# A fused attention and two-layer kernel: fixed places for all SBUF tiles, and tiles of their own for one batch's remaining keys and values

## The chip, the cores and the metric

The kernel runs on one core of one Trainium2 chip. The metric is device time in microseconds (us) for one execution. The core's engines are TensorE (PE, with its weight loads shown apart as PEld), VectorE (DVE), ScalarE (ACT), GpSimd (POOL) and SyncE (SP). Here SP issues all transfers between HBM and SBUF.

## The reference

The reference is linear attention with a norm, followed by two two-layer blocks, all in float32. The shapes are 8 batches, 8 heads, 576 positions and head size 64, and then 4608 tokens, model width 512 and hidden width 2048.

```python
kv = np.einsum('bhsd,bhse->bhde', k, v)
out = np.einsum('bhsd,bhde->bhse', q, kv)
rms = np.sqrt(np.mean(out * out, axis=-1, keepdims=True) + 1e-06)
x = (out / rms * g_norm)            # then to (4608, 512)
h = x @ w_in1;  g = h * (1.0 / (1.0 + np.exp(-1.702 * h)));  y = g @ w_out1
h = y @ w_in2;  r = np.maximum(h, 0.0);  out = (s * (r * r) + b) @ w_out2
```

## The kernel before, in words

Every float32 operand of the large products is split into a high and a low part (`xh`, `xl`; `wih`, `wil`; `gh`, `gl`; the two halves of `wo`), and three matmuls (high by high, low by high, high by low) stand for one product. The three have lines of their own: L424 to L426 in the first layer's first product (`mm1`), L453 to L455 in its second (`mm2`), L520 to L522 and L616 to L618 in the second layer. In each of these matmuls the first-named SBUF operand in the code is the stationary one (loaded as weights, 128 columns) and the second the moving one (512 columns).

**First layer.** The 4608 tokens are nine blocks of 512. A step of the main loop (`for n in range(2, ...)`, L931) takes one of 16 slices of the hidden width for one block: 12 matmuls of `mm1` on the block's transposed input, then 12 matmuls of `mm2` of the step two before. Blocks 0 and 1 alternate in parts at the beginning, while their weights come in; the others take 16 steps each. A block's input lies in `xh0` and `xl0` if its number is even and in `xh1` and `xl1` if it is odd (`x_tiles`, L337). Beside these steps the attention of the next block runs: `kv_pair` (keys by values, L222), `att_u` (queries, L297), the norm and the transposition of four tiles of 128 tokens; `tile_at` (L662) says in which step each part of a tile stands.

**Second layer.** The second layer's first product is done by a scheme with seven block products in place of eight (`product`, L507). It works on 4 couples of blocks and one single block, each in 8 pairs of hidden slices. Its weights are the stationary operand. They are loaded in halves that go round `xh1`, `xl1`, `xl0` (`load_half`, L489), and the moving operand is in the tiles that held `wih` and `wil`, or in `xh0`. Between the products stand the second product's matmuls (`units`, L594): stationary is the activation, which lies in places listed in `G_PLACE` (for pairs of even number `wraw`, `kt`, `vt`; for pairs of odd number `q`, `xn0` and `xn1`, `wf0` and `wf1`, `gh`), moving is `wo`. A pair has 42 matmuls of the first kind and 48 of the second.

**The beginning, written out by hand (L764 to L921).** For each batch the first 512 positions of keys and values come as four pairs of tiles (`load_kv`, L211), the other 64 as one pair of tiles `krem`, `vrem` (`load_rem`, L205), of which there is one pair for all batches. All transfers go through SP in the order in which they are written. `kv_pair` multiplies a pair's four chunks and then the remaining rows. Batch 0's four pairs (`kv_first`) end with the remaining rows, so `load_rem(1)` stands behind the last of them, at L808, after the loads of batch 1's four pairs. `kv_pair(1, 0)` stands at L832, and behind it on PE the transposition of the third tile (`att_turn(2)`), on ACT `x_first(2)`, on DVE `xl_first(2)`. From L763 on `keep_warm` puts matmuls of no use into gaps.

**Where the tiles lie.** Tiles of the pool `sb` lie one behind the other in each partition, in the order in which their names are first taken in the program. A tile of 512 numbers has 2048 bytes per partition, the larger ones 4096 or 8192; `ms0` to `ms3` and `r0` to `r3` have 8 numbers, 32 bytes. The names are first taken in this order: `kt0 vt0 q0 kt1 vt1 q1 wraw0 yf0 yf1 yf4 yf2 yf3 yf5 wraw1 xn0 | ms0 r0 | wf0 xn1 | ms1 r1 | xh0 xl0 xo0 xo1 wst wc yf6 wf1 | ms2 r2 ms3 r3 | wih0 wil0 wf2 wih1 wil1 g0 wo0 gh0 xh1 xl1 g1 gl0 ...` and then all others. So, counted in bytes beyond a multiple of 256 from the first tile, `kt0` to `xn0` start at 0, `wf0` and `xn1` at 64, `xh0` to `wf1` at 128, and all from `wih0` on, `xh1` and `xl1` among them, at 0 again. The slices that the large matmuls read are multiples of 256 bytes into their tiles.

Of the kernel before, what the change touches and what calls it, by code (L numbers as in the profile page):

```python
# [16 lines left out]
P = 128  # L17
B, H, S, D = 8, 8, 576, 64
# [4 lines left out]
BT = 512  # L23
NB = NT // BT
TT = BT // P
# [2 lines left out]
CUTS = (0, 2, 6, 11, KF)  # L28
HEAD = [(j, lo, hi) for lo, hi in zip(CUTS, CUTS[1:]) for j in range(2)]
PARTS = HEAD + [(j, 0, KF) for j in range(2, NB)]  # L30
WARM = 8
SM = 512
NC = SM // P
# [9 lines left out]
def tile_attn_moe_moe2(  # L43
# [18 lines left out]
    nc = tc.nc  # L62
# [7 lines left out]
    def new(tag, shape=(P, BT), dtype=F32, name=None):  # L70

        return sb.tile(list(shape), dtype, tag=tag, name=name or tag)

    def rot(tag, n, shape=(P, BT), dtype=F32, name=None):

        turns[tag] = turns.get(tag, -1) + 1
        return new(f"{tag}{turns[tag] % n}", shape, dtype, name or tag)

    def move(dst, src):

        raw = [x.bitcast(F32) if x.dtype == F32R else x for x in (dst, src)]
        nc.sync.dma_start(out=raw[0], in_=raw[1])
# [14 lines left out]
    rem_t = {nm: const.tile([P, H * D], F32, name=f"{nm}rem") for nm in "kv"}  # L97
# [7 lines left out]
    def load_w(which, ph, f):  # L105
        raw = rot("wraw", 2, (P, DM, 2), U32)
        nc.sync.dma_start(out=raw.rearrange("p a b -> p (a b)"), in_=w_arg[ph][which][f].bitcast(U32))
        w_raw[which, ph, f] = raw

    def to_f32(which, ph, f):  # L110

        raw = w_raw.pop((which, ph, f))
        lo, hi = raw[:, :, 0], raw[:, :, 1]
        w = rot("wf", 3, (P, DM), U32)
        nc.scalar.activation(out=w.bitcast(F32), in_=hi.bitcast(F32), func=ACTF.Abs)
        nc.scalar.activation(out=lo, in_=lo, func=ACTF.Copy, scale=2.0 ** -29)
        yield

        nc.vector.tensor_scalar(
            out=w.bitcast(F32), in0=w.bitcast(F32), scalar1=W_LEAST, scalar2=W_MOST, op0=ALU.max, op1=ALU.min
        )
        yield
        nc.vector.tensor_scalar(
            out=w, in0=w, scalar1=3, scalar2=0x3FFFFFF8, op0=ALU.logical_shift_left, op1=ALU.bitwise_and
        )
        yield
        nc.vector.scalar_tensor_tensor(
            out=w, in0=hi, scalar=0xC0000000, in1=w, op0=ALU.bitwise_and, op1=ALU.bitwise_or  # L130
        )
        yield
        nc.vector.tensor_tensor(out=w, in0=w, in1=lo, op=ALU.add)
        w_raw[which, ph, f] = w.bitcast(F32)
        yield
# [66 lines left out]

    kt, vt, rem = {}, {}, {}

    def load_rem(bb):  # L205
        for nm, src in (("k", k_rest), ("v", v_rest)):

            nc.sync.dma_start(out=rem_t[nm][0:S - SM], in_=src[bb])
            rem[nm, bb] = rem_t[nm]

    def load_kv(bb, p, place=None):  # L211
        for nm, src, dst, hl in (("kt", k, kt, 0), ("vt", v, vt, 1)):
            if place is None:
                t = rot(nm, 2, (P, NC, P))
            else:
                t = new(place[hl], (P, NC, P))
            nc.sync.dma_start(out=t, in_=src[bb, p].rearrange("p (c e) -> p c e", e=P))
            dst[bb, p] = t
# [66 lines left out]
    def load_q(i, place=None):  # L285
        if place is None:
            q_t[i] = rot("q", 2, (P, NP, P))
        else:
            q_t[i] = new(place, (P, NP, P))
        nc.sync.dma_start(out=q_t[i], in_=q[i].rearrange("p (a t) -> p a t", t=P))  # L290
# [20 lines left out]
    def att_sq(i, place=None):  # L311
        if place is None:
            xn_t[i] = rot("xn", 2, (P, H, D))
        else:
            xn_t[i] = new(place, (P, H, D))
        nc.scalar.activation(out=xn_t[i], in_=u_t[i], func=ACTF.Square, scale=D ** -0.5)
# [43 lines left out]
    y_dram = {}  # L360
    for j, lo, _ in PARTS:
        y_dram.setdefault(j, {})[lo] = dp.tile([KD, P, BT], F32, name=f"y{j}_{lo}")
# [44 lines left out]

    steps = [(j, f, lo, hi) for j, lo, hi in PARTS for f in range(lo, hi)]
    begin = {}
# [245 lines left out]
    def at(n, slot, fn, *args):  # L655
        beside.setdefault((n, slot), []).append((fn, args))
# [5 lines left out]
    def tile_at(i, n, n_norm, n_turn, slot="turn"):  # L662

        at(n, "pe", att_u, i)
        at(n, "act", att_sq, i)
        at(n, "r", att_r, i)
        at(n_norm, "norm", att_norm, i)
        at(n_turn, slot, att_turn, i)
        early = "0" if slot == "pe" else ""
        at(n_turn, "xh" + early, att_xh, i)  # L670
        at(n_turn, "xl" + early, att_xl, i)
# [10 lines left out]
    def next_kv(bb, n):  # L682
        at(n, "load", load_rem, bb)
        for p in range(2):
            at(n, "load", load_kv, bb, p)

    at(5, "load", load_rem, 2)
    for p in range(2):
        at(7 + 2 * p, "load", load_kv, 2, p)

    n0 = begin[1, CUTS[-2]]
# [4 lines left out]
    tile_at(2 * TT, n0 - 2, n0 - 1, n0, "pe")  # L696
    tile_at(2 * TT + 1, n0 - 1, n0, n0)
    tile_at(2 * TT + 2, n0 + 1, n0 + 2, n0 + 2)
    tile_at(2 * TT + 3, n0 + 1, n0 + 2, n0 + 2)

    for v_ in range(3, NB):
        n0 = begin[v_ - 1, 0]
# [37 lines left out]
    for n in range(2 * KF, NB * KF):  # L740
        j, f = divmod(n, KF)
# [5 lines left out]
            at(n - RING + 2, "load", load_wo, 0, f)  # L747

    with tc.manual_schedule():
        make_identity(nc, ident)  # L750
        for t in rem_t.values():
            nc.gpsimd.memset(t[S - SM:P], 0.0)
        for t in kvbd:
            nc.gpsimd.memset(t, 0.0)
# [5 lines left out]
        def keep_warm(n):  # L760
            for _ in range(n):
                nc.tensor.matmul(o[:, 0:P], ident, ident, start=True, stop=True)

        keep_warm(WARM)  # L764
        load_kv(0, 0)
        load_rem(0)
        load_q_pair(0, "q0")
        load_kv(0, 1)
# [21 lines left out]
        keep_warm(5)  # L790
        next(ci0)
        att_sq(1, xn_place[1])
        load_kv(1, 0)
        load_kv(1, 1)
        kv_first(2)
# [9 lines left out]
        u_first(2)  # L805
        load_kv(1, 2, ("xo0", "xo1"))
        load_kv(1, 3, ("wst", "wc"))
        load_rem(1)  # L808
        load_q(4)
        load_q(5)  # L810
        kv_first_out(3)
# [253 lines left out]
```

## Time and profile before

| what | value |
|---|---|
| three runs | 1650.14 us median (1649.44 to 1652.71) |
| the profiled execution | 1650.09 us |
| its span, first to last instruction | 1648.3 us |
| PE busy | 1631.0 us (99%), 8008 matmuls |
| DVE, ACT, POOL busy | 912.1 us (55%), 665.3 us (40%), 68.7 us (4%) |
| the chain that ended last, by engine | PE 95%, DMA 2%, DVE 1%, ACT 1% |
| granted TensorE clock, mean | 0.996 |
| transfers | 375.75 MB, mean 228 GB/s |

The profile has one line for each group of instructions; in `out<-in` the buffers' numbers are left out, so `xl` is `xl0` or `xl1`. PE busy counts a matmul from its start to its modelled end; these overlap, so the pace of the engine is read from the starts. The granted clock is 1.00 at 2.4 GHz and 0.50 at 1.2 GHz.

### The profile page before, as it was taken

The numbers are of one execution on the slowest core, as the hardware profiler recorded it, in microseconds if no ns is written. First come the engines' busy times: TensorE is split into PE (matmuls) and PEld (weight loads), VectorE is DVE, ScalarE is ACT, GpSimd is POOL, SyncE is SP. The second block draws the span as 40 slices with busy tenths as digits, with TensorE's granted clock in tenths as the row PEclk, the third lists the DMA queues.
The fourth block names the chain that finished last, engine by engine and source line by source line (L and its number), as shares of the span: only waits on it lengthen the run. The fifth ranks groups of instructions, "written<-read, shape, count | busy, mean of one in ns | idle before, by whom it ended". The sixth has DMA issues, their size and how long they took to land.

```text
span 1648.3 us, 21336 instructions
## 1 busy us (share of the span) xinstructions
PE 1631.0 (99%) x8008; PEld 1343.7 (82%) x8008; DVE 912.1 (55%) x1520; ACT 665.3 (40%) x1164; POOL 68.7 (4%) x47
## 2 busy tenths in 40 slices
PE   8999999999999999999999999999999999999999
PEld 6788788888888888888888888888888888888888
DVE  5876636656666545665534655555455455445443
ACT  4665533443444433443323433333333333333343
POOL 3000100001000000100000000000000000000000
PEclk9999999999999999999999999999999999999999
DMA  6566757687787766776588844974486448544773
GB/s 230 188 227 199 243 178 248 238 298 267 270 300 294 275 211 222 251 269 210 190 316 281 312 155 167 317 243 153 142 288 222 140 142 292 191 140 142 251 278 140
DMA packets 126775, 375.75 MB, mean 228 GB/s; under 512 B 14417, under 2 KB 20049, under 8 KB 121169
## 3 DMA queue, kind: packets, MB, share of 16 engines
q1 hardware_dynamic: 126672, 374.40, 65.2%
q8 instruction: 63, 1.03, 0.3%
q14 instruction: 40, 0.32, 0.1%
HBM read 284.69 MB, written 89.65 MB: 227 GB/s over the span
## 4 chain that ended last, share of the span: by engine, by line
PE 95%; DMA 2%; DVE 1%; ACT 1%; issue 0%; SPq 0%; ACTq 0%; DVEq 0%
PE acc L453 8%; PE h L424 8%; PE h L426 8%; PE acc L455 8%; PE h L425 8%; PE acc L454 8%; PE sum L616 4%; PE sum L617 4%; PE sum L618 4%; PE A L520 4%; PE A L521 4%; PE A L522 4%; PE z L618 4%; PE z L616 4%; PE z L617 4%; PE D L522 2%
## 5 line engine op out<-in xcount | busy, mean ns | idle before, releaser
L453 PE MATMUL acc<-gh,wo 128*128 128x512 f32 x576 | 230.0, 399 | 1.0 <-ACT ev L463 1.0
L424 PE MATMUL h<-xh,wih 128*128 128x512 f32 x576 | 229.1, 398 | 0.0
L426 PE MATMUL h<-xl,wih 128*128 128x512 f32 x576 | 226.5, 393 | 0.0
L425 PE MATMUL h<-xh,wil 128*128 128x512 f32 x576 | 226.1, 393 | 0.0
L455 PE MATMUL acc<-gl,wo 128*128 128x512 f32 x576 | 225.5, 391 | 0.0
L454 PE MATMUL acc<-gh,wo 128*128 128x512 f32 x576 | 225.4, 391 | 0.0
L431 ACT ACTIVATE g<-h 128x512 f32<-128x512 f32 x144 | 86.0, 597 | 274.2 <-PE h L426 273.9
L432 DVE TENSOR_TENSOR g<-g,h 128x512 f32<-128x512 f32 x144 | 98.8, 686 | 162.5 <-ACT g L431 162.2
L436 ACT CAST gh<-g 128x512 fp32r<-128x512 f32 x144 | 89.5, 622 | 138.1 <-DVE g L432 138.1
L453 PEld LDWEIGHTS acc<-gh,wo 128*128 128x128 f32 x576 | 108.8, 189 | 25.0 <-ACT ev L463 1.4
L426 PEld LDWEIGHTS h<-xl,wih 128*128 128x128 f32 x576 | 108.4, 188 | 24.7
L425 PEld LDWEIGHTS h<-xh,wil 128*128 128x128 f32 x576 | 108.6, 188 | 23.3
L455 PEld LDWEIGHTS acc<-gl,wo 128*128 128x128 f32 x576 | 108.6, 188 | 23.2
L424 PEld LDWEIGHTS h<-xh,wih 128*128 128x128 f32 x576 | 108.4, 188 | 22.7
L454 PEld LDWEIGHTS acc<-gh,wo 128*128 128x128 f32 x576 | 108.7, 189 | 21.5
L440 DVE TENSOR_TENSOR gl<-g,gh 128x512 fp32r<-128x512 f32 x144 | 98.9, 687 | 27.3 <-PE acc L455 26.2
L323 POOL TENSOR_TENSOR r<-ms,mhalf 128x8 f32<-128x8 f32 x36 | 66.0, 1838 | 721.6 <-DVE ms L322 721.6
L565 DVE TENSOR_TENSOR wst<-B,wst 128x512 f32<-128x512 f32 (+1 forms) x40 | 25.5, 639 | 108.2 <-PE B L522 108.1
L520 PE MATMUL A<-wih,xl 128*128 128x512 f32 (+1 forms) x212 | 78.7, 371 | 0.2 <-ACT wst L562 0.2
L522 PE MATMUL A<-wil,xl 128*128 128x512 f32 (+1 forms) x212 | 78.5, 370 | 0.0
L521 PE MATMUL A<-wih,xl 128*128 128x512 f32 (+1 forms) x212 | 78.4, 370 | 0.0
L626 DVE TENSOR_TENSOR g<-z,g 128x512 f32<-128x512 f32 x56 | 38.7, 692 | 56.4 <-PE z L618 55.8
(241 smaller groups left out, 3144.6 us busy)
## 6 DMA issues: line engine op xcount, KB each, us to landing
wo<-wo SPq DMA_DIRECT2D x208, 512.0 KB, 4.9
x<-xo SPq DMA_DIRECT2D x56, 512.0 KB, 4.0
xl<-wi SPq DMA_DIRECT2D x26, 1024.0 KB, 5.3
xl<-wi SPq DMA_DIRECT2D x27, 768.0 KB, 4.7
wraw<-in_w_in SPq DMA_DIRECT2D x32, 512.0 KB, 4.5
wraw<-in_w_out SPq DMA_DIRECT2D x32, 512.0 KB, 4.2
y<-ev SPq DMA_DIRECT2D x60, 256.0 KB, 2.7
yf<-y SPq DMA_DIRECT2D x60, 256.0 KB, 5.1
```

Of the source, the lines that this page charges most:

```text
L424: nc.tensor.matmul(o, wh[:, cs], xh[:, c, :], start=(c == 0), stop=False)
L425: nc.tensor.matmul(o, wl[:, cs], xh[:, c, :], start=False, stop=False)
L426: nc.tensor.matmul(o, wh[:, cs], xl[:, c, :], start=False, stop=(c == KD - 1))
L453: nc.tensor.matmul(o, wh[:, ds_], gh, start=(f == lo), stop=False)
L454: nc.tensor.matmul(o, wl[:, ds_], gh, start=False, stop=False)
L455: nc.tensor.matmul(o, wh[:, ds_], gl, start=False, stop=(f == hi - 1))
L520: nc.tensor.matmul(o, wh, xh, start=(c == 0 and not more), stop=False, skip_group_check=more)
L521: nc.tensor.matmul(o, wl, xh, start=False, stop=False, skip_group_check=more)
L522: nc.tensor.matmul(o, wh, xl, start=False, stop=(c == 1), skip_group_check=more)
L616: nc.tensor.matmul(o, gh[:, cs], wh, start=begins, stop=False)
L617: nc.tensor.matmul(o, gh[:, cs], wl, start=False, stop=False)
L618: nc.tensor.matmul(o, gl[:, cs], wh, start=False, stop=ends)
```

## The change

A list `PLACES` names all tiles of the pool, and a new function takes each of them once, at the beginning and in this order. The eight small tiles stand together in it, behind `wf0` and ahead of `xh0`. Batch 1's remaining rows go to two new tiles in the places of `ev0` and `ev1` (free until the first partial result is written), are cleared beside the old pair on POOL, and are loaded ahead of batch 1's first pair rather than behind its last. The fourth tile of block 2 (`2 * TT + 3`) has its `att_u`, norm and transposition one step later each.

```diff
+PLACES = (
+    "kt0 vt0 kt1 vt1 yf0 yf1 yf2 yf3 q0 q1 wraw0 yf4 yf5 wraw1 xo0 xo1 wst wc xn0 xn1 yf6 wf0 "
+    "ms0 r0 ms1 r1 ms2 r2 ms3 r3 xh0 xl0 wih0 wil0 wf1 wih1 wil1 wf2 g0 gh0 wih2 wil2 g1 gh1 "
+    "wo0 gl0 xh1 xl1 wih3 wil3 gl1 gh2 wo1 wo2 wo3 ev0 ev1 ev2 ev3 wih4 wil4 wih5 wil5 wih6 wil6 "
...
+    def lay_out():
+        sizes = {"wraw": 1024, "xo": 1024, "wst": 1024, "wc": 1024, "wo": 1024, "xh": 2048, "xl": 2048, "ms": H, "r": H}
+        for tag in PLACES.split():
+            new(tag, (P, sizes.get(tag.rstrip("0123456789"), BT)))
...
-    def load_rem(bb):
+    def load_rem(bb, place=rem_t):
         for nm, src in (("k", k_rest), ("v", v_rest)):
-            nc.sync.dma_start(out=rem_t[nm][0:S - SM], in_=src[bb])
-            rem[nm, bb] = rem_t[nm]
+            nc.sync.dma_start(out=place[nm][0:S - SM], in_=src[bb])
+            rem[nm, bb] = place[nm]
...
-    tile_at(2 * TT + 3, n0 + 1, n0 + 2, n0 + 2)
+    tile_at(2 * TT + 3, n0 + 2, n0 + 3, n0 + 3)
...
     with tc.manual_schedule():
+        lay_out()
         make_identity(nc, ident)
-        for t in rem_t.values():
+        rem_t1 = {nm: new(f"ev{i}", (P, H * D), name=f"{nm}rem1") for i, nm in enumerate("kv")}
+        for t in (*rem_t.values(), *rem_t1.values()):
             nc.gpsimd.memset(t[S - SM:P], 0.0)
...
         att_sq(1, xn_place[1])
+        load_rem(1, rem_t1)
         load_kv(1, 0)
...
         load_kv(1, 3, ("wst", "wc"))
-        load_rem(1)
         load_q(4)
```

## Rows read from the trace of the kernel before

**Rows 1.** Windows: us, busy of PE, PEld, DVE, ACT, POOL, clock, DMA share, GB/s.
```profile
24.50:31.30 6.80, 5.09 (x34) 4.07 (x35) 2.77 (x5) 1.91 (x3) 0.00 (x0) 0.50 0.41 140
```

**Rows 2.** Timeline of PE: start, us, instruction, count, idle before and its releaser.
```profile
21.39 0.69 PE L236 MATMUL kvps<-vt,kt 128*64 128x64 f32 x16
26.21 0.48 PE L236 MATMUL kvps<-vrem,krem 128*64 128x64 f32 x4 [4.14 <-DMA vrem<-in_v_rest]
...
64.64 0.50 PE L453 MATMUL acc<-gh,wo 128*128 128x512 f32 x1 [0.98 <-ACT ev L463]
```

**Rows 3.** Timeline of SP's queue: batch 1's first keys, the remaining values, first output weights.
```profile
12.94 0.33 SPq L217 DMA_DIRECT2D kt<-in_k  x1
...
20.23 0.48 SPq L208 DMA_DIRECT2D vrem<-in_v_rest  x1
...
22.55 0.33 SPq L107 DMA_DIRECT2D wraw<-in_w_out  x1
```

**Rows 4.** DMA view, transfers issued at 13.69 and 22.55: KB, us to landing.
```profile
vt<-in_v SPq DMA_DIRECT2D x1, 256.0 KB, 6.5
...
wraw<-in_w_out SPq DMA_DIRECT2D x1, 512.0 KB, 5.9
```

**Rows 5.** Timelines of DVE and of ACT behind the late rows.
```profile
28.50 0.75 DVE L281 SCALAR_TENSOR_TENSOR xl<-xtp,g,xh 128x512 fp32r<-128x512 f32 x1 [3.61 <-ACT xh L276]
...
32.87 0.75 DVE L281 SCALAR_TENSOR_TENSOR xl<-xtp,g,xh 128x512 fp32r<-128x512 f32 x1 [1.96 <-ACT xh L276]
...
28.45 0.68 ACT L117 ACTIVATE wf<-wraw 128x512 f32<-128x512 f32 x1
```

**Rows 6.** Timeline of POOL: a clear of 64 rows, and the four norms of block 1.
```profile
1.83 0.52 POOL L752 MEMSET vrem<- 64x512 f32 x1
...
38.46 6.64 POOL L323 TENSOR_TENSOR r<-ms,mhalf 128x8 f32<-128x8 f32 x4 [14.41 <-DVE ms L322]
```

**Rows 7.** Timeline of PE: `mm1`'s first matmul and `mm2`'s, blocks 4 and 5.
```profile
471.04 0.40 PE L424 MATMUL h<-xh,wih 128*128 128x512 f32 x1
...
473.83 0.39 PE L453 MATMUL acc<-gh,wo 128*128 128x512 f32 x1
...
568.35 0.39 PE L424 MATMUL h<-xh,wih 128*128 128x512 f32 x1
...
571.07 0.39 PE L453 MATMUL acc<-gh,wo 128*128 128x512 f32 x1
```

**Rows 8.** Timeline of PE: six matmuls with weights in `xl1`, six in `xl0`.
```profile
1082.55 0.39 PE L520 MATMUL A<-wih,xl 128*128 128x512 f32 x1
...
1083.91 0.39 PE L616 MATMUL sum<-wo,wraw 128*128 128x512 f32 x1
...
1092.08 0.40 PE L520 MATMUL A<-wih,xl 128*128 128x512 f32 x1
...
1093.47 0.39 PE L616 MATMUL sum<-wo,wraw 128*128 128x512 f32 x1
```

**Rows 9.** Windows, as rows 1: blocks 4 and 5, then 29 pairs.
```profile
420.84:518.71 97.87, 97.87 (x522) 79.47 (x520) 61.60 (x109) 45.63 (x82) 7.78 (x4) 1.00 0.80 286
518.71:615.17 96.46, 96.46 (x514) 79.57 (x513) 54.90 (x94) 39.26 (x69) 6.91 (x4) 1.00 0.74 265
948.00:1545.64 597.64, 597.64 (x2611) 490.34 (x2610) 307.37 (x458) 213.49 (x345) 0.00 (x0) 1.00 0.57 198
```

**Rows 10.** Timeline of PE, pair 13 in `units`: stationary `q`, `gh`, then `wf`, `xn`.
```profile
1192.46 0.40 PE L616 MATMUL sum<-wo,q 128*128 128x512 f32 x1
...
1193.86 0.39 PE L616 MATMUL z<-wo,wf 128*128 128x512 f32 x1
...
1195.25 0.39 PE L520 MATMUL A<-wih,xh 128*128 128x512 f32 x1
```

**Rows 11.** Timeline of PE: first `mm2` matmuls behind a group of small ones.
```profile
147.88 0.50 PE L453 MATMUL acc<-gh,wo 128*128 128x512 f32 x1
148.22 0.39 PE L454 MATMUL acc<-gh,wo 128*128 128x512 f32 x1
```

More of the change, by code (lines that the diff above doesn't have):

```diff
@@ L30 @@
 PARTS = HEAD + [(j, 0, KF) for j in range(2, NB)]
+PLACES = (
[5 rows of a table added]
+)
 WARM = 8
```

2 rows, old and new, of the table PLACES are left out of this document.

## The prediction

> **What bounds the kernel now.** I read the page first: PE is busy for 1631.0 of 1648.3 us, and the chain that ended last is 95% PE. DVE (55%), ACT (40%) and the transfers stand beside it. So only two things can move the end: time in which PE waits, and the pace at which PE takes one matmul after the other. I looked for both.
>
> The waits of PE come next, by the timeline of its instructions. They lie nearly all in the first 65 us. The longest is 4.14 us: `kv_pair(1, 0)` starts at 21.39, does its four chunks, and stands until 26.21 for batch 1's remaining values [rows 2]. The windows say what that does to the clock: it was granted in full up to that idle stretch, and from 24.5 to 31.3 it is at 0.50, the 1.2 GHz level [rows 1]. The last wait of this part is 0.98 us at 64.64 for ACT [rows 2]; from there PE is the bound.
>
> Then the pace, by the starts of matmuls of one form in places where nothing waits. The 12 matmuls of `mm1` take 473.83 - 471.04 = 2.79 us in block 4, 232.5 ns each, and 571.07 - 568.35 = 2.72 us in block 5, 226.7 ns each [rows 7]. Same instructions, same shapes, no idle time, clock at 1.00 in both blocks [rows 9]. What differs is that block 4's input lies in `xh0` and `xl0`, block 5's in `xh1` and `xl1`. In the second layer six product matmuls with weights in `xl1` take 1083.91 - 1082.55 = 1.36 us, 226.7 ns each, and six with weights in `xl0` 1093.47 - 1092.08 = 1.39 us, 231.7 ns each [rows 8]. Again only the tile differs.
>
> **What the places have to do with it.** Counted by sizes in the order of first use, `xh0` and `xl0` start 128 bytes beyond a multiple of 256 from the first tile, while `xh1`, `xl1`, all `wih`, `wil`, `gh`, `gl` and `wo` start at a multiple. My reading: a matmul whose two SBUF operands differ in their place by a multiple of 256 bytes takes 226.7 ns, any other some 5 to 6 ns more. It also fits the sums: `wf` and `xn` as stationary (places 64 and 128 off, `xn0` alone on the line) take 1195.25 - 1193.86 = 1.39 us for six, 231.7 ns each [rows 10]. The six before, with `q` and `gh`, which are on the line, take 1.40 us [rows 10]; they follow a product with weights in `xl0`, so a slow matmul seems to slow its neighbours. In the new list the eight 32-byte tiles, 256 bytes in all, stand together, so every tile that a large matmul reads is on one line. No pair of places arises that the kernel before doesn't have at its fast pace somewhere.
>
> The Trainium skill speaks against this: "TensorE: Matmul & The Clock Gate", section "Step-by-step: what each phase is for", gives PE two independent read ports and says that the next weights' load takes nothing from the running matmul, and "SBUF — State Buffer", section "Who interferes with whom", that PE waits on nobody. By these rules the places are worth nothing; rows 7 and 8 disagree, with 232.5 against 226.7 ns. What the change would come to by them is rival B.
>
> **The places, step by step.** First layer, upper bound: block 4 takes 97.87 us, block 5 96.46 [rows 9], 1.41 us more; that is more than 16 times the 0.07 us of one step's `mm1` [rows 7], so all slices have it, wherever their weights lie, and `mm2` has a little. Three such blocks (2, 4, 6) make 4.2 us; block 8 (16 steps) and block 0 (14 steps after the start) have no like neighbour, so 30 x 0.07 = 2.1. Together 6.3. Lower bound: `mm1` alone, and nothing in the four steps of a block that follow a transposition: (3 x 12 + 30) x 0.07 = 4.6.
>
> Second layer, upper bound: 29 pairs hold 2610 matmuls in 597.64 us, 229.0 ns each [rows 9]. At 226.7 that is 2.3 x 2880 = 6.6 us for the 32 full pairs; the eight half-wide pairs count nothing. Lower bound, only matmuls that are off the line themselves, at 5.0 ns [rows 8, 10]: weights in `xl0`, a third of 42 x 32 = 448; `xh0` as moving operand with weights elsewhere, some 96; `wf` and `xn`, 24 in each of 16 odd pairs, 384. Together 928 x 5.0 = 4.6 us.
>
> So the places bring 9.2 to 12.9 us. I take 11.0, the middle, since the rows show the neighbours slowed but not all of them. All of it lies on PE where PE is the bound, so nothing hides it. What would be late next has room: DVE at 55%.
>
> **The remaining rows.** Now they are issued at 20.23 and wait in the queue behind batch 1's eight tiles [rows 3]. In the new order they take the slots from 12.94 on [rows 3], and everything that stood between moves back by 256 KB. The queue takes a slot of that size each 13.69 - 12.94 = 0.75 us [rows 3, 4]. So the first pair's values land at 13.69 + 6.5 + 0.75 = 20.9 [rows 4], before PE wants them at 21.39 [rows 2]; the cover is 0.5 us, and if it is gone the cost is what is missing from it. The whole 4.14 us of PE go then, but not as a gain. Behind the rows stands the first output weights' load: issued at 22.55, landing 5.9 later at 28.45 [rows 3, 4], where ACT's conversion starts in the same instant [rows 5]. The transfers ahead of it are the same in sum, so it stays there, and on ACT `x_first(3)` stands behind this conversion's two instructions. 28.45 and three ACT instructions of 0.66 give 30.4 for `xl_first(3)` on DVE, which now starts at 32.87 [rows 5]. From there DVE and POOL's train of norms (6.64 us from 38.46 [rows 6]) set the pace up to 64.64, and move as a whole. Gain: 32.87 - 30.4 = 2.4 us.
>
> Bounds: nothing, if the clock falls again (PE now idles for some 2 us ahead of 30.4, and a late `att_u` would hold the train of norms where it is); 4.1 us, the wait itself, if the load lands earlier (DVE idled 3.61 and 1.96 us [rows 5], so there is room). I take 2.4, to which the landing points.
>
> Two clears more on POOL, 0.52 us each [rows 6], stand ahead of the `kvbd` clears and of the small tile that ACT's warm-up instruction reads. Nobody else waits for POOL until the first norm; I cost them at nothing. Without that cover: 1.0 us at most. The list itself issues no instruction.
>
> **The fourth tile of block 2** makes two groups of small matmuls out of one, in two steps. Behind a group `mm2`'s first matmul takes 148.22 - 147.88 = 0.34 us rather than 0.23 [rows 11]. One more such place before `mm2` and one before `mm1`: 0.2 us more, between 0 and 0.4. No wait of PE goes with it; the block begins three steps later, so the tile is still in time.
>
> **Sum.** Against the profiled execution, 1650.09 us, which is 1.8 above its span and within 0.1 of the median: 1650.1 - 11.0 - 2.4 + 0.2 = 1636.9 us.
>
> **Rivals.** A: the places work, the early rows bring nothing, by the clock or since the first pair's values land too late: 1650.1 - 11.0 + 0.2 = 1639.3. For it: after each long idle stretch of this part PE could run at 0.50 again, as in rows 1.
>
> B: the places do nothing, and what differs between even and odd blocks is something that I don't see (the change doesn't do what its first part says): 1650.1 - 2.4 + 0.2 = 1647.9. Against it: two different operations show the same 5 to 6 ns, once with the tile moving, once stationary.
>
> C, slower: what counts is not the remainder by 256 but the two operands' distance in some larger unit. The new order moves `xh1` and `xl1` by 10 KB, so they could come to lie as badly as `xh0` and `xl0` do now, and those stay bad. Blocks 1, 3, 5, 7 have 60 steps after the start: 60 x 0.07 = 4.2; two thirds of the products, 896 x 5.0 = 4.5. That gives 1650.1 + 8.7 - 2.4 + 0.2 = 1656.6. It decides once `mm1` of an odd block takes 2.79 us. Against it: a block's 16 slices have weights at 16 distances, and rows 9 say that all are alike.
>
> **How the numbers follow.** Forecast 0.72, A 0.08, B 0.13, C 0.05, neither part of any effect (1650.3) 0.02. A measurement of this kernel can tell about 0.2%, 3.3 us, from no change. The forecast and A are faster by more: 0.80; B and the last are within: 0.15; C is slower: 0.05. The range takes the bounds: 1650.1 - 12.9 - 4.1 = 1633 at the low end, 1650.1 - 9.2 + 0.4 = 1641.3, so 1641, at the high end; A lies in it.
>
> **What the new profile would show.** Places: 12 matmuls of `mm1` take 2.72 us in even blocks too, blocks 4 and 5 are as long as each other, pairs take 20.4 to 20.5 us. Rows: no wait before `kv_pair(1, 0)`'s remaining rows, `xl_first(3)` at about 30.4, ACT's first output conversion still at 28.4, PE's wait for `ev` at about 62.2. The prediction is wrong if even blocks stay at 2.79 us, or if ACT's conversion moves with the rows.

## The result, and the profile of the kernel after

| | before | after |
|---|---|---|
| time, 5 runs each on one chip | 1649.44 us (1648.83 to 1652.71) | 1634.1 us (1633.61 to 1635.7) |
| ratio | | 0.9906, 95% interval 0.9891 to 0.992 |
| span of the profiled execution | 1648.3 us | 1631.9 us |

The forecast was 1636.9 us, 1633 to 1641. The kernel is faster, and its time is 2.8 us under the forecast. Timed a second time beside other runs (`after_again`), it took 1634.88 us, ratio 0.9911 (0.9897 to 0.9926).

The 16.4 us between the two spans lie in these stretches. Their borders are the starts of the same matmul in both timelines of PE.

| stretch | before | after | gain |
|---|---|---|---|
| start to the end of PE's wait for `ev` | 64.64 | 60.24 | 4.40 |
| from there to block 2 | 161.88 | 160.70 | 1.18 |
| blocks 2 to 7 | 579.15 | 575.99 | 3.16 |
| block 8 and the first three pairs | 142.33 | 140.61 | 1.72 |
| 29 pairs | 597.64 | 591.60 | 6.04 |
| the rest | 102.66 | 102.76 | -0.10 |

Line numbers behind the new function are 13 higher than before: `mm1` is L437 to L439, `mm2` L466 to L468, the product L533 to L535, the units L629 to L631.

First the beginning, by the timeline of PE, the queue of SP, and the timelines of ACT, DVE and POOL; these answer to [rows 2, 3, 5, 6].

```profile
20.88 0.69 PE L249 MATMUL kvps<-vt,kt 128*64 128x64 f32 x16
21.36 0.32 PE L249 MATMUL kvps<-vrem,krem 128*64 128x64 f32 x4
...
60.24 0.50 PE L466 MATMUL acc<-gh,wo 128*128 128x512 f32 x1 [1.42 <-ACT ev L476]
```
```profile
12.71 0.47 SPq L221 DMA_DIRECT2D krem<-in_k_rest  x1
13.57 0.47 SPq L221 DMA_DIRECT2D vrem<-in_v_rest  x1
...
21.49 0.33 SPq L120 DMA_DIRECT2D wraw<-in_w_out  x1
```
```profile
27.47 0.68 ACT L130 ACTIVATE wf<-wraw 128x512 f32<-128x512 f32 x1 [3.29 <-DMA wraw<-in_w_out]
...
29.32 0.75 DVE L294 SCALAR_TENSOR_TENSOR xl<-xtp,g,xh 128x512 fp32r<-128x512 f32 x1 [0.70 <-ACT xh L289]
...
34.80 6.53 POOL L336 TENSOR_TENSOR r<-ms,mhalf 128x8 f32<-128x8 f32 x4 [11.41 <-DVE ms L335]
```

The remaining rows are asked for 6.7 us earlier (13.57 against 20.23), and the 4.14 us of PE ahead of them are gone. ACT now stands 3.29 us for the first output weights, which land at 27.45. Before they landed at 28.42 [rows 4], just as `x_first(2)` ended on ACT. Everything behind moves forward as a train: `xl_first(3)` on DVE from 32.87 to 29.32, the norms on POOL from 38.46 to 34.80, the end of PE's last wait from 64.64 to 60.24.

The clock, by windows (columns as in [rows 1]). Before, two stretches were at 0.50, the 1.2 GHz level: 24.49 to 31.32 [rows 1] and 44.97 to 51.80 (the first line here). After, the first is gone (second line) and the other is shorter, 43.45 to 46.86 (third line, whose window is set 0.1 us too late). Ahead of this one PE had stood 2.13 us for DVE before and 2.14 after.

```profile
44.97:51.80 6.83, 5.78 (x17) 4.60 (x18) 6.59 (x12) 2.40 (x4) 0.14 (x1) 0.50 0.35 129
```
```profile
24.50:31.30 6.80, 5.67 (x59) 3.81 (x57) 4.13 (x8) 3.60 (x8) 0.00 (x0) 1.00 0.68 244
...
43.56:46.98 3.42, 3.42 (x10) 2.49 (x9) 3.32 (x7) 1.71 (x3) 0.00 (x0) 0.52 0.48 158
```

What the clock does to PE here shows in the last transposition of block 1's input (four matmuls), before and then after:

```profile
47.11 1.09 PE L333 MATMUL xtp<-ident,yf 128*128 128x128 f32 x4 [0.17 <-DVE yf L327]
```
```profile
42.94 0.63 PE L346 MATMUL xtp<-ident,yf 128*128 128x128 f32 x4 [0.63 <-DVE yf L340]
```

It takes 1.09 us inside the stretch at 0.50, and 0.63 us where it ends just ahead of one.

Then the pace, by the timeline of PE, for blocks 4 and 5 (first `mm1` and first `mm2` of a step), weights in `xl1` (at 1070.83) and in `xl0` (at 1080.35), and six units with `wf` and `xn` (at 1145.62); these answer to [rows 7, 8, 10].

```profile
464.00 0.39 PE L437 MATMUL h<-xh,wih 128*128 128x512 f32 x1
...
466.72 0.39 PE L466 MATMUL acc<-gh,wo 128*128 128x512 f32 x1
...
560.78 0.39 PE L437 MATMUL h<-xh,wih 128*128 128x512 f32 x1
...
563.50 0.39 PE L466 MATMUL acc<-gh,wo 128*128 128x512 f32 x1
...
1070.83 0.39 PE L533 MATMUL A<-wih,xl 128*128 128x512 f32 x1
...
1072.18 0.39 PE L629 MATMUL sum<-wo,wraw 128*128 128x512 f32 x1
...
1080.35 0.39 PE L533 MATMUL A<-wih,xl 128*128 128x512 f32 x1
...
1081.70 0.39 PE L629 MATMUL sum<-wo,wraw 128*128 128x512 f32 x1
...
1145.62 0.39 PE L629 MATMUL z<-wo,wf 128*128 128x512 f32 x1
...
1146.98 0.39 PE L533 MATMUL A<-wih,xl 128*128 128x512 f32 x1
```

`mm1` takes 2.72 us in both blocks, 226.7 ns for each matmul. Six product matmuls take 1.35 us with weights in either tile, and six units with `wf` and `xn` take 1.36 us rather than 1.39. Everything that was slow before has the pace of what was fast. The windows of blocks 4 and 5 and of the 29 pairs, as in [rows 9], say the same in sum:

```profile
414.35:511.13 96.78, 96.78 (x521) 79.44 (x520) 61.49 (x109) 45.58 (x82) 7.78 (x4) 1.00 0.81 290
511.13:607.55 96.42, 96.42 (x513) 79.57 (x512) 54.80 (x94) 39.25 (x69) 7.34 (x4) 1.00 0.74 266
937.54:1529.14 591.60, 591.60 (x2611) 489.86 (x2610) 307.34 (x458) 213.43 (x345) 0.00 (x0) 1.00 0.59 200
```

Block 4 is 1.09 us shorter and block 5 0.04. A pair takes 591.60 / 29 = 20.40 us. Block 4 keeps 0.36 us over block 5; its window holds eight matmuls more (x521 against x513), as it did before (x522 against x514 in [rows 9]).

### The profile page after: what moved, and what is told of

It reads as the page before. It is cut to its first block, busy times and chain, and to the rows that moved or that the text cites. A ratio compares the mean times of both kernels' runs of the same rounds, so it can differ in the third digit from the quotient of the medians.

```text
span 1631.9 us, 21340 instructions
## 1 busy us (share of the span) xinstructions
PE 1614.0 (99%) x8008; PEld 1338.4 (82%) x8008; DVE 911.3 (56%) x1520; ACT 664.1 (41%) x1164; POOL 70.3 (4%) x49
## 4 chain that ended last, share of the span: by engine, by line
PE 95%; DVE 2%; DMA 1%; ACT 1%; issue 0%; SPq 0%; ACTq 0%; DVEq 0%
PE acc L466 8%; PE acc L468 8%; PE acc L467 8%; PE h L437 8%; PE h L438 8%; PE h L439 8%; PE sum L629 4%; PE sum L630 4%; PE sum L631 4%; PE A L533 4%; PE A L535 4%; PE A L534 4%; PE z L629 4%; PE z L630 4%; PE z L631 4%; PE D L535 2%
## 5 line engine op out<-in xcount | busy, mean ns | idle before, releaser
L466 PE MATMUL acc<-gh,wo 128*128 128x512 f32 x576 | 229.8, 399 | 1.4 <-ACT ev L476 1.4
L437 PE MATMUL h<-xh,wih 128*128 128x512 f32 x576 | 227.3, 395 | 1.1 <-ACT xh L289 1.1
L468 PE MATMUL acc<-gl,wo 128*128 128x512 f32 x576 | 225.3, 391 | 0.0
L467 PE MATMUL acc<-gh,wo 128*128 128x512 f32 x576 | 225.2, 391 | 0.0
L439 PE MATMUL h<-xl,wih 128*128 128x512 f32 x576 | 224.5, 390 | 0.1
L438 PE MATMUL h<-xh,wil 128*128 128x512 f32 x576 | 224.4, 390 | 0.0
L466 PEld LDWEIGHTS acc<-gh,wo 128*128 128x128 f32 x576 | 108.6, 188 | 24.6 <-ACT ev L476 1.8
L468 PEld LDWEIGHTS acc<-gl,wo 128*128 128x128 f32 x576 | 108.5, 188 | 23.6 <-DVE gl L453 0.7
L439 PEld LDWEIGHTS h<-xl,wih 128*128 128x128 f32 x576 | 108.1, 188 | 23.4 <-DVE xl L294 0.5
L437 PEld LDWEIGHTS h<-xh,wih 128*128 128x128 f32 x576 | 108.2, 188 | 22.9 <-ACT xh L289 1.2
L438 PEld LDWEIGHTS h<-xh,wil 128*128 128x128 f32 x576 | 108.3, 188 | 21.7 <-DVE wil L162 0.3
L467 PEld LDWEIGHTS acc<-gh,wo 128*128 128x128 f32 x576 | 108.6, 189 | 20.9
L533 PE MATMUL A<-wih,xl 128*128 128x512 f32 (+1 forms) x212 | 78.1, 368 | 0.2 <-ACT wst L575 0.2
L535 PE MATMUL A<-wil,xl 128*128 128x512 f32 (+1 forms) x212 | 77.8, 367 | 0.0
```

Of the source, the lines that this page charges most:

```text
L437: nc.tensor.matmul(o, wh[:, cs], xh[:, c, :], start=(c == 0), stop=False)
L438: nc.tensor.matmul(o, wl[:, cs], xh[:, c, :], start=False, stop=False)
L439: nc.tensor.matmul(o, wh[:, cs], xl[:, c, :], start=False, stop=(c == KD - 1))
L466: nc.tensor.matmul(o, wh[:, ds_], gh, start=(f == lo), stop=False)
L467: nc.tensor.matmul(o, wl[:, ds_], gh, start=False, stop=False)
L468: nc.tensor.matmul(o, wh[:, ds_], gl, start=False, stop=(f == hi - 1))
```

## The experiments

**The places alone.** The kernel before with only the list and the function that takes it; rows and tile as they were.

```diff
+PLACES = ("kt0 vt0 kt1 vt1 ... wih15 wil15")     # the list of the change
+    def lay_out(): ...
     with tc.manual_schedule():
+        lay_out()
```

> The kernel before with the new list of places and nothing else; rows and tile stay as they were. If the remainder of the places counts: mm1 takes 2.72 us in even blocks too, pairs 20.40 us, the beginning is unchanged with 4.1 us of waiting for the remaining values; time about 12 us under before, 1637.5. If the gain came with the early rows instead (PE's pace kept up by something that begins there): 1649 and even blocks at 2.79 us.

Measured: 1637.4 us (1636.71 to 1640.14) against 1650.44, ratio 0.9919 (0.9902 to 0.9935). PE's wait for the late rows and the window of the pairs:

```profile
25.80 0.48 PE L249 MATMUL kvps<-vrem,krem 128*64 128x64 f32 x4 [4.43 <-DMA vrem<-in_v_rest]
```
```profile
941.77:1533.37 591.60, 591.60 (x2611) 489.86 (x2610) 307.42 (x458) 213.44 (x345) 0.00 (x0) 1.00 0.58 200
```

The wait is still there, and the pairs have the pace of the kernel after to the hundredth. So the list by itself brings about 13.0 us, and it issues no instruction.

**The rows alone.** The changed kernel with the names in the order of the kernel before, and the tile's old step.

```diff
-PLACES = ("kt0 vt0 kt1 vt1 yf0 yf1 ...")
+PLACES = "kt0 vt0 q0 kt1 vt1 q1 wraw0 yf0 yf1 yf4 yf2 yf3 yf5 wraw1 xn0 ms0 r0 wf0 xn1 ms1 r1 xh0 xl0 ..."
-    tile_at(2 * TT + 3, n0 + 2, n0 + 3, n0 + 3)
+    tile_at(2 * TT + 3, n0 + 1, n0 + 2, n0 + 2)
```

> The changed kernel with all tiles at the places that the kernel before gave them (its order of first use, written as the list) and the fourth tile of block 2 in its old step: only the early rows are left. If the two parts are independent: mm1 of even blocks back at 2.79 us, pairs at 20.46 to 20.71, the first wait for ev ends at about 60.2 us as in the changed kernel rather than at 64.6; time about 4.3 us under before, 1645.1. If the beginning's extra 2 us over the 2.4 predicted come from the places: the wait ends at about 62.2 and the time is 1647.

Measured: 1647.76 us (1645.44 to 1649.31) against 1650.44, ratio 0.9978 (0.9969 to 0.9988). ACT's first output conversion, PE's last wait of the beginning, and the windows of block 4 and of the pairs:

```profile
28.84 0.66 ACT L124 ACTIVATE wf<-wraw 128x512 f32<-128x512 f32 x1 [4.36 <-DMA wraw<-in_w_out]
...
62.79 0.50 PE L460 MATMUL acc<-gh,wo 128*128 128x512 f32 x1 [1.96 <-ACT ev L470]
```
```profile
419.65:517.52 97.87, 97.87 (x521) 79.46 (x520) 61.59 (x109) 45.51 (x82) 7.78 (x4) 1.00 0.79 286
...
946.82:1544.47 597.65, 597.65 (x2612) 490.30 (x2610) 307.29 (x458) 213.50 (x345) 0.00 (x0) 1.00 0.57 198
```

Block 4 and the pairs are back at the times of [rows 9]: calling all names at the beginning does nothing, their order does. The rows bring 2.7 us here. PE's wait ends at 62.79 and not at the 60.2 that was expected of two independent parts: the figures are those of the rival, by which the places help the beginning. But the run with 256 bytes below has the new places and ends this wait at 62.54, so the places are not what makes the difference; more on it in the section on the prediction. The two parts add up: 13.0 + 2.7 = 15.7, and both together brought 1649.44 - 1634.1 = 15.3.

**What of the place counts: 128 bytes, and 256.** Two kernels tell a tile's own place from its distance to the other operand, and the unit of that distance. In both an unused tile stands ahead of `xh0`, so that `xh0`, `wih0` and all behind them move by 128 or by 256 bytes against `kt0` to `wf0` and the small tiles. In the first layer both operands move, in the units of the second layer one of them.

```diff
-    "ms0 r0 ms1 r1 ms2 r2 ms3 r3 xh0 xl0 wih0 wil0 ...
+    "ms0 r0 ms1 r1 ms2 r2 ms3 r3 pad0 xh0 xl0 wih0 wil0 ...     # pad: 32 numbers, or 64
```

> The changed kernel with 128 bytes of unused room ahead of xh0, so that xh0, xl0 and all tiles behind them move together. If the two operands' difference counts: first layer and products keep 226.7 ns, since both operands moved; only units' matmuls with weights in kt, vt, wraw, q, xn or wf0 are off against wo, some 42 of 48 in each of 32 pairs at 5 ns or a little more, so 1641 to 1643. If a tile's own place counts (a start that suits the engine by itself): all large matmuls run at 231 to 233 ns, 30 us or more over the changed kernel, 1664.

> The changed kernel with 256 unused bytes ahead of xh0, where the run with 128 had its pairs at 20.79 us and 1646.7 us in all. Theory: what counts is the remainder of the distance between the two operands by 256 bytes, so that this shift does nothing: pairs at 20.40 us, the products and units at 226.7 to 227.5 ns, the time about 1634. Rival: a larger unit (512 bytes or more) counts, and the second layer is slow as with 128: pairs at 20.8 us, units above 229 ns, about 1647.

Measured: 1646.7 us with 128 bytes and 1635.9 us with 256, in one execution each. First 128 bytes, windows of block 4 and of the pairs, and starts of six units with `wraw` and `vt` and the product behind them; then 256 bytes, the same windows:

```profile
414.57:511.42 96.85, 96.85 (x521) 79.46 (x520) 61.58 (x109) 45.60 (x82) 7.78 (x4) 1.00 0.81 292
...
938.85:1541.85 603.00, 603.00 (x2611) 490.78 (x2610) 307.72 (x458) 213.70 (x345) 0.00 (x0) 1.00 0.57 196
```
```profile
1159.25 0.40 PE L629 MATMUL sum<-wo,wraw 128*128 128x512 f32 x1
...
1160.64 0.39 PE L533 MATMUL D<-wih,xh 128*128 128x512 f32 x1
...
1162.01 0.40 PE L629 MATMUL z<-wo,kt 128*128 128x512 f32 x1
```
```profile
416.48:513.26 96.78, 96.78 (x522) 79.46 (x520) 61.51 (x109) 45.43 (x82) 7.78 (x4) 1.00 0.81 292
...
939.67:1531.27 591.60, 591.60 (x2612) 489.87 (x2611) 307.34 (x458) 213.26 (x345) 0.00 (x0) 1.00 0.58 200
```

With 128 bytes `mm1` keeps its pace, although `xh`, `wih` and `wil` have all moved: moving a tile by 128 bytes together with the other operand does nothing. The units, whose operands now differ by 128, take 1.39 us for six, and the pairs 20.79 us. With 256 bytes nothing is slow. So it is the difference of the two operands' places, modulo 256 bytes. These runs don't tell whether it is a matmul's own two operands that count, or its moving operand and the weights of the next one.

The price was expected too low (1641 to 1643 us). The products behind the units have both operands on one line, and yet six of them take 1162.01 - 1160.64 = 1.37 us, 228.3 ns each; over the 29 pairs products took 229.3 ns in the mean, and units from 229.2 ns (with `q` and `gh`) to 234.9 (with `wf` and `xn`). A pair loses (603.00 - 591.60) / 29 = 0.39 us, and 32 of them 12.6 us, which is 1646.7 - 1634.1. In an even pair all 48 units are off the line, which makes 0.39 us / 48 = 8 ns each; in an odd pair 32 are (those with `gh` and `wf1` are not), which makes 12 ns each. That is with what they do to the matmuls behind them, and more than the 5 to 6 ns of one alone.

**The curve between 0 and 256.** The changed kernel with all `wih` and `wil` at the end of the list and small unused tiles between them. Slices 0 to 7 have both 0, 32, 64 ... 224 bytes off; slices 8 to 15 have `wih` on the line and `wil` 0 to 224 off.

```diff
+    "wo7 wih0 wil0 pad1 wih1 wil1 pad2 wih2 wil2 ... pad7 wih7 wil7 pad8 wih8 wih9 ... wih15 wil8 pad9 wil9 pad10 wil10 ... wil15"
```

> The changed kernel with the first layer's weights at the end of the pool, 32 bytes of unused room between one slice's pair and the next: slices 0 to 7 have wih and wil 0, 32, 64 to 224 bytes off the line; slices 8 to 15 have wih on the line and wil 0 to 224 off. xh and xl stay on the line, so each step's mm1 shows the price of one difference. If only equality counts: 2.72 us for slice 0 and the same 2.79 us or so for slices 1 to 7, and for 9 to 15 with only one matmul of three off about a third to the whole of that. If a smaller unit than 256 counts (64 or 128), slices 2, 4, 6 or slice 4 are at 2.72 us too; the kernel before showed only 64 and 128 off.

Measured: 1656.16 us, in one execution. Starts of the first `mm1` and `mm2` of four steps in block 8 (here L438 and L467): slices 0, 3, 6 and 8, that is 0, 96, 192 and 0 bytes off.

```profile
807.42 0.39 PE L438 MATMUL h<-xh,wih 128*128 128x512 f32 x1
...
810.14 0.39 PE L467 MATMUL acc<-gh,wo 128*128 128x512 f32 x1
...
823.93 0.39 PE L438 MATMUL h<-xh,wih 128*128 128x512 f32 x1
...
826.74 0.40 PE L467 MATMUL acc<-gh,wo 128*128 128x512 f32 x1
...
840.59 0.39 PE L438 MATMUL h<-xh,wih 128*128 128x512 f32 x1
...
843.34 0.39 PE L467 MATMUL acc<-gh,wo 128*128 128x512 f32 x1
...
851.58 0.39 PE L438 MATMUL h<-xh,wih 128*128 128x512 f32 x1
...
854.30 0.39 PE L467 MATMUL acc<-gh,wo 128*128 128x512 f32 x1
```

The steps take 2.72, 2.81, 2.75 and 2.72 us. The mean from one start to the next over the `mm1` matmuls of each slice, leaving out the places where small matmuls stand between them:

| bytes off | 0 | 32 | 64 | 96 | 128 | 160 | 192 | 224 |
|---|---|---|---|---|---|---|---|---|
| `wih` and `wil` off, ns | 226.7 | 232.9 | 233.2 | 234.2 | 232.9 | 233.2 | 229.8 | 232.6 |
| only `wil` off, ns | 226.7 | 232.4 | 230.8 | 232.3 | 231.2 | 233.3 | 231.1 | 231.5 |

Each of these differences costs, 3 to 7.5 ns, with no order in it; only 0 is free. With one matmul of three off the line, the group loses nearly as much as with all three. And behind a slow `mm1` the matmuls of `mm2`, all on the line here, are slow too for up to eight matmuls: behind slice 5 of blocks 2 to 8 the first eight take 224 to 236 ns each, 231.5 in the mean, and the ninth 227. What happens inside PE for such a pair of places isn't seen in any row and stays open.

**Slot or tile.** The change gives the remaining rows both an earlier slot in SP's queue and tiles of their own. Here they have the tiles but the old slot.

```diff
-        load_rem(1, rem_t1)
         load_kv(1, 0)
...
         load_kv(1, 3, ("wst", "wc"))
+        load_rem(1, rem_t1)
```

> The changed kernel with batch 1's remaining rows in their own tiles, but loaded in the old slot of the queue, behind the eight tiles of keys and values. If the slot counts (theory): the wait of some 4 us before kv_pair(1, 0)'s remaining rows is back, the wait for ev ends near 64.6 rather than 60.2, time 3 to 4 us over the changed kernel. If the old pair's reuse was what held the load back: it lands earlier all the same, and the time stays within 1 us of the changed kernel.

Measured: 1638.67 us (1637.69 to 1639.94), ratio 0.9934 (0.9919 to 0.9949). Timeline of PE:

```profile
26.78 0.48 PE L249 MATMUL kvps<-vrem,krem 128*64 128x64 f32 x4 [4.82 <-DMA vrem<-in_v_rest]
...
65.00 0.50 PE L466 MATMUL acc<-gh,wo 128*128 128x512 f32 x1 [1.25 <-ACT ev L476]
```

The wait is back in full. The slot is what counts. That the old tiles would not allow the early slot follows from the code, where batch 0's last two pairs still read them; it was not run.

**The fourth tile's step.** The changed kernel with `tile_at(2 * TT + 3, n0 + 1, n0 + 2, n0 + 2)`, as before.

> The changed kernel with the fourth tile of block 2 in its old step. By the sum: two first matmuls behind small groups less, 0.2 us less from 190 to 220 us, which is under what the time can tell. Rival: the later step takes a wait out of block 1's last steps that the trace of before doesn't show; then this is slower by that wait.

Measured: 1634.87 us (1633.69 to 1636.48), ratio 0.9908 (0.9892 to 0.9925). The changed steps lie between block 0's last step and block 2's first. Timeline of PE, this kernel and then the changed one:

```profile
186.62 0.39 PE L437 MATMUL h<-xh,wih 128*128 128x512 f32 x1
...
223.83 0.39 PE L437 MATMUL h<-xh,wih 128*128 128x512 f32 x1
```
```profile
183.65 0.39 PE L437 MATMUL h<-xh,wih 128*128 128x512 f32 x1
...
220.94 0.39 PE L437 MATMUL h<-xh,wih 128*128 128x512 f32 x1
```

37.21 against 37.29 us. The step costs 0.08 us, which the times can't tell from nothing. In this profile PE stood 2.71 us for queries at 181.28 (1.33 in after), ahead of the stretch that is compared. With the old step it is 1.39 in the run of the rows alone and in the next one, so the longer wait doesn't belong to the step.

**The first output weights earlier, and later queries earlier.** Two kernels try to go on from what the profile of after shows. Both keep the tile's old step and load the first output weights ahead of the queries of tiles 4 and 5. The second also asks for the queries of tiles 8 and 9 five steps earlier, since PE stands for the first of them (1.33 us near 180 in after, 1.49 before).

```diff
-        load_q(4)
-        load_q(5)
...
+        load_q(4)
+        load_q(5)                                   # behind the first output weights
...
-    for t, n in enumerate((-4, -3, -2, -1)):
+    for t, n in enumerate((-9, -8, -2, -1)):        # the second kernel only
```

> As e6, and the first output weights are loaded ahead of the queries of tiles 4 and 5 rather than behind them. If their landing is what sets the beginning's end now (ACT's conversion starts as it lands): it starts about 1.2 us earlier, at about 26.3, and xl_first(3), the train of norms and the wait for ev move by 1.0 to 1.2 us; time about 1 us under e6. If something else holds (the wait for norms on POOL or the clock): the conversion moves and the wait for ev stays at 60.2.

> The changed kernel with the fourth tile's step as before, the first output weights loaded ahead of the queries of tiles 4 and 5, and the queries of tiles 8 and 9 asked for five steps earlier. In the profile of the changed kernel PE stands 1.3 to 1.5 us near 178 us for the queries of tile 8, and the same stall stands in the kernel before. Theory: that transfer starts too late, and an earlier start takes the stall away with nothing behind it, so the step it lies in goes from some 8 to 6.6 us and the time to about 1632.0, against 1633.4 without it. Rival: the transfer shares its queue with the loads of values and weights for the second batch, another of them comes late instead, and the time stays at 1633 to 1635.

Measured: 1633.36 us (1632.64 to 1633.93), ratio 0.9901 (0.9887 to 0.9916), and 1634.01 us (1632.23 to 1636.3), ratio 0.9904 (0.9887 to 0.992). Neither can be told from the changed kernel. First kernel, ACT and PE; then the second, ACT twice and PE:

```profile
27.62 0.68 ACT L130 ACTIVATE wf<-wraw 128x512 f32<-128x512 f32 x1 [3.13 <-DMA wraw<-in_w_out]
...
180.41 1.13 PE L318 MATMUL u<-kvbd,q 128*128 128x128 f32 x8 [1.39 <-DMA q<-in_q]
```
```profile
26.21 0.67 ACT L130 ACTIVATE wf<-wraw 128x512 f32<-128x512 f32 x1 [1.90 <-DMA wraw<-in_w_out]
...
178.52 0.66 ACT L130 ACTIVATE wf<-wraw 128x512 f32<-128x512 f32 x1 [2.89 <-DMA wraw<-in_w_out]
...
186.18 0.50 PE L467 MATMUL acc<-gh,wo 128*128 128x512 f32 x1 [1.12 <-DVE wo L162]
```

In the first profile the weights landed at 27.60, no earlier than in after, against what was expected; in the second they landed at 26.18, and PE's wait for `ev` ended at 59.06, the earliest of all. The stall for the queries is gone in the second, but the rival held: an output weight comes late instead, ACT converts it 2.89 us after it could have, and PE stands 1.12 us for its low half at 186.18. From the step at 169.11 to block 2 at 219.69 it takes 50.58 us, without the earlier queries 50.65. The earlier queries made it no shorter. That the transfers of this stretch set its length whatever their order is argued from these two executions, not shown.

## Why the prediction held, and where it was off

**The places: right in mechanism, 0.9 us too small.** The forecast was 11.0, within 9.2 to 12.9. Behind PE's wait for `ev` the spans give 12.0, or 11.9 without the tile and a stall for queries: in the first layer 1.18 + 3.16 + 1.39 (block 8 alone) = 5.7, close to the middle of 4.6 to 6.3; in the second layer 16.4 - 4.4 - 5.7 = 6.3, close to the upper bound of 6.6 rather than to the middle. The term that was mis-sized is the neighbours. The lower bound counted only matmuls that are off the line themselves, and the middle was taken since "the rows show the neighbours slowed but not all of them". But the second layer's upper bound was a measurement, the mean of 229.0 ns over 29 pairs [rows 9], and all of its excess over 226.7 went. The 128-byte run shows why: what is off the line costs 8 to 12 ns there, not 5.0, with the matmuls behind it.

In the first layer the middle came out by two errors that cancel. The 1.41 us between blocks 4 and 5 were put down to the places, but 0.36 of them stay in the kernel after, where both blocks have one pace: block 4 has eight matmuls more [rows 9]. Without these, three blocks make 3.2 in place of 4.2, and blocks 2 to 7 gave 3.16. On the other side a step costs more than its `mm1`: in block 8 steps went from 5.53 to 5.44 us, 0.09 and not 0.07, and the block gave 1.39 where 16 x 0.07 = 1.1 was counted.

**The remaining rows: the wait went as forecast, the gain was larger in the profile.** No wait stands ahead of the rows, and the slots are those from 12.7 on. "The transfers ahead of it are the same in sum, so it stays there" is the step that failed: the first output weights landed at 27.45, not at 28.45, and ACT's conversion came with them. By the prediction's own sign ("if ACT's conversion moves with the rows") this part was wrong in the profiled execution. The step behind it held: 27.47 and three ACT instructions of 0.66 give 29.45, and `xl_first(3)` started at 29.32. The runs with the rows late, then those with the rows early:

| us | weights issued | landed | ACT converts | `xl_first(3)` | norms | wait for `ev` ends |
|---|---|---|---|---|---|---|
| before | 22.55 | 28.42 | 28.45 | 32.87 | 38.46 | 64.64 |
| places alone | 21.11 | 28.06 | 28.08 | 33.07 | 38.70 | 64.86 |
| old slot | 21.66 | 29.02 | 29.05 | 33.18 | 38.76 | 65.00 |
| after | 21.49 | 27.45 | 27.47 | 29.32 | 34.80 | 60.24 |
| after, again | 22.39 | 26.67 | 26.69 | 29.01 | 34.59 | 60.75 |
| tile's old step | 21.25 | 27.19 | 27.21 | 29.06 | 34.54 | 60.19 |
| 128 bytes | 21.41 | 27.34 | 27.36 | 29.20 | 34.69 | 60.34 |
| 256 bytes | 22.78 | 28.68 | 28.70 | 30.52 | 36.38 | 62.54 |
| rows alone | 22.95 | 28.82 | 28.84 | 30.67 | 36.63 | 62.79 |
| curve | 23.96 | 27.25 | 27.68 | 30.58 | 36.18 | 62.33 |
| weights earlier | 20.22 | 27.60 | 27.62 | 29.48 | 34.96 | 60.63 |
| weights and queries earlier | 20.48 | 26.18 | 26.21 | 28.06 | 33.54 | 59.06 |

With late rows `xl_first(3)` is at 33, whatever the weights do. With early rows it follows ACT's conversion by 1.8 to 1.9 us, as the forecast has it, but for two executions (after again, the curve) in which `x_first(3)` also waited 0.35 and 0.94 us for PE. So with early rows the landing of the weights sets the pace in most executions, and it varies: 26.7 to 28.8 with one and the same queue. It doesn't follow the time of issue. With late rows it was 28.1 to 29.0 in three executions; whether the change itself brings it forward, and what makes it vary, is open.

The train behind `xl_first(3)` doesn't quite move as a whole either. From there to the end of the wait it is 31.77 us before and 30.92 after, and 30.9 to 32.1 over all runs. The clock has a part in it: the last transposition of block 1 took 1.09 us before and 0.63 in the profile of after, where the clock fell to 0.50 at 43.45, just behind it. That was luck of this execution; in seven of the other eight with early rows it took 1.08 or 1.09. Of the 4.40 us in the profile 2.4 are the forecast's, some 1.1 come from the earlier landing, and 0.85 from the shorter train. The bound of 4.1 took the wait itself as the most that could be won, and put nothing in for either.

**Rival A's clock half** came in part, in two of the nine executions with early rows. In the run with 256 bytes and in that of the rows alone PE stood 1.31 and 1.24 us for the first pair's values, the clock fell once more, at 30.39 to 33.80 and 30.80 to 34.21, and the wait for `ev` ended only 2.1 and 1.9 us earlier than before. The window of the rows alone:

```profile
30.80:34.20 3.40, 3.40 (x14) 2.19 (x16) 3.33 (x6) 2.70 (x6) 0.00 (x0) 0.50 0.02 8
```

In both the weights were late too, so how much of it is the clock's is not shown. The cover of 0.5 us ahead of the first pair's values was as thin as forecast: in four of the runs with early rows PE stood 0.7 to 1.9 us for them. Where it stood 0.70 (128 bytes) and 1.88 (weights earlier) the clock did not fall there, and the wait for `ev` ended at 60.34 and 60.63.

The times agree with a gain of this size: by the ratios, moving the rows to their old slot costs 3.8 to 4.6 us, the rows alone bring 3.6 (2.7 by the medians), and the changed kernel gains 1.3 to 2.1 on the places alone. Each is uncertain by some 2 to 4 us.

**The tile** was costed at 0.2 and took 0.08 us.

**The other rivals.** B, that the places do nothing, fell with the run of the places alone: 1637.4 us against 1650.44 for the kernel before. The Trainium skill gives PE two independent SBUF read ports, in "TensorE: Matmul & The Clock Gate", section "Step-by-step: what each phase is for". In "SBUF — State Buffer", section "Who interferes with whom", it says that PE never waits on anyone. Taken as rules for the pace, these would have made B right; here the same matmul takes 226.7 or 232.9 ns by where its two operands lie to each other, and the measurement decides. Whether a read port or something else is behind it, no run shows. C, a larger unit, fell with odd blocks that stay at 2.72 us, and with the run of 256 bytes.

**In sum** the span lost 3.2 us more than the forecast's 13.2: 2.0 from the rows, 0.9 from the places, 0.1 from the tile, and 0.1 to 0.2 from a stall for queries that was a little shorter.

## What to carry to other kernels

Where the same matmul has two paces in one profile, sort the starts by the tiles that it reads; then put all matmul operands on one line modulo 256 bytes, by gathering the small tiles in a block whose size is a multiple of that, since it costs no instruction. Size such a gain by the mean pace of the whole stretch against the best pace seen, and not by the slow instructions alone; and see that the two stretches hold the same instructions. Where loads are moved in a queue, don't take the landing of what stands behind them as fixed: read it from several executions of the same kernel, and ask whether its consumer waits for it or for its own engine.

## What the runs showed of the hardware

- A 128x512 float32 matmul (128 columns of weights) starts 226.7 ns after the one before if the SBUF places of its weights and of its moving operand differ by a multiple of 256 bytes, and 229.8 to 234.2 ns after it, in the mean of a slice's 12, at any of the seven other multiples of 32. A shift of both together by 128 bytes did nothing.
- A slow matmul slows those behind it: `mm2` on the line for up to eight matmuls, and the products beside the units off the line to 229.3 ns in the mean.
- The clock's low stretches (0.50) differ between executions of one kernel. In the two profiles of the changed kernel it stood at 43.45 to 46.86 in one, and at 8.36 to 15.19 and 42.49 to 49.32 in the other; the times of the two agree within 0.1%. All twelve profiles have one that begins between 41.8 and 46.0.
- Four transposing matmuls (128x128 float32) in a row take 0.63 us with the clock at 1.00 and 1.09 us at 0.50.
